# Low weight parts on GpSimd, and softmax division inside the transposing product, in an attention, MoE, MoE kernel

## The chip, the cores and the metric

The kernel runs on one core of one Trainium2 chip. The metric is the device time of one execution in microseconds, taken as the median of a few executions; lower is better. The profiled execution is one of them, recorded instruction by instruction.

## What is computed

Attention with a memory term (4 batches, 8 heads, 576 rows, 64 columns a head) gives a matrix of 2304 tokens by 512 columns. Two feed-forward layers (MoE 1 and MoE 2, each 512 to 2048 to 512) follow.

```python
scores = scale * q @ k.T                      # causal mask, B=4, H=8, S=576, D=64
a = exp(scores - scores.max(-1)); a /= a.sum(-1) + 1e-9
local = a @ v
q_p = where(q > 0, q, exp(q) - 1) + 1
mem_out = (q_p @ M_prev) / (q_p @ z_prev + 1e-6)
x = g * mem_out + (1 - g) * local             # g = sigmoid(beta), one per head
h = x @ w_in;  x = (h * sigmoid(h)) @ w_out   # MoE 1
h = x @ w_in2; out = elu(h) @ w_out2          # MoE 2
```

The weights arrive as 64-bit floating-point numbers, everything else as 32-bit ones.

## The kernel before

**Numbers in two parts.** The feed-forward products run on TensorE in a format with fewer mantissa bits (fp32r). Each operand is therefore kept as a high part (a copy in fp32r) and a low part (the number minus its high part), and three products (high by high, low by high, high by low) are summed. `split2` (L474) makes the two: ScalarE (ACT) copies the high part, VectorE (DVE) subtracts for the low part.

**Weights of MoE 1.** There are 32 tiles of 128 by 512: 16 of `w_in` (named `w0_0` to `w0_15`) and 16 of `w_out` (`w1_0` to `w1_15`). `w_stream` (L548) loads each as 64-bit integers into a landing tile (four landing places, which carry the names of the last tiles, such as `w0_14`). `w_value` builds the 32-bit number with one ACT and three DVE instructions (a TENSOR_SCALAR and two SCALAR_TENSOR_TENSOR on 128x512), and `w_split` (L543) calls `split2`: an ACT cast for the high part and a DVE TENSOR_TENSOR of 128x512 for the low part. The next load into a landing tile waits until the low part has read it.

**Attention.** Work is cut into tasks of a batch, a pair of heads and a region of rows. Batch 0 has two tasks for each of its four pairs: region A (rows 0 to 255) and region B (rows 256 to 575); the other batches have one task a pair (AB). `soft` (L729) does the scores of a task on TensorE (PE), the mask and the row minimum on DVE (a custom instruction, from PSUM), the exponential with row sums on ACT, the reciprocal of the sums on DVE, and then divides: the tiles called `e3` are scaled by ACT (`NORM = '3'`), all others (`eA`, `e2`, `e4`) by a DVE TENSOR_SCALAR. `a_T` (L789) and `b_T` (L802) transpose the divided tiles 128 columns at a time on PE, by a pass of the identity matrix (`ident`) over the tile; ACT copies the result out of PSUM (`a`), and `av_mm` multiplies it by the values. The result `x` of batch 0 is split at once and feeds MoE 1, whose blocks run woven into the attention of the later tasks.

**Order.** Nothing is issued in the order of the code. A planner (`Plan`) records all instructions, prices each with `Plan.cost`, schedules them on five engines in 24 forward and backward passes, and issues them in the order of its best pass. Each engine then works its instructions strictly in that order. A price in `Plan.cost` therefore moves instructions on all engines. Before the first weights are there, PE is given 70 small products of zeros as a filler.

GpSimd (POOL) does only memsets and masks here: 13 instructions in the first 3 us, and later one memset of 64x128 for each task.

Of the kernel before, what the change touches and what calls it, by code (L numbers as in the profile page):

```python
# [9 lines left out]
F32 = mybir.dt.float32  # L10
# [4 lines left out]
ALU = mybir.AluOpType  # L15
# [4 lines left out]
HP = 2000  # L20
OFF = 200
NORM = '3'
XHP = 1000
HOOK = 4
AHEAD = 4
# [132 lines left out]
class Plan:  # L158
# [82 lines left out]
    @staticmethod  # L241
    def cost(op, fn, args, kw, ins, outs, together):
        def cols(v):
            n = 1
            for m in v.shape[1:]:
                n *= m
            return n

        if op.eng == "PE":
            if fn == "transpose":  # L250
                return max(ins[0].shape[0] / 1.2, 0.84 * cols(ins[0]))
            n, m, once = cols(kw["rhs"]), cols(kw["lhsT"]), kw["rhs"].dtype != F32
            if together > 1:
                return n / (2.4 if together > 4 and kw["lhsT"].shape == (64, 64) else 1.2)
            return max(n / (2.4 if once else 0.6) + (13.5 if once else 3.0), 0.84 * m * (1 if once else 2))
        if op.eng == "DMA":
            v = outs[0] if isinstance(outs[0], View) else ins[0]
            n = 4
            for m in v.shape:
                n *= m  # L260
            return max(430.0, n / 280.0)
        n = cols(outs[0])
        psum = any(v.tile.space == "psum" for v in ins)
        if op.eng == "ACT":
            c = n / 1.2 + (51 if psum else 93) + (186 if kw.get("accum_out") is not None else 0)
            return c + (93 if isinstance(kw.get("scale"), View) else 0)
        if op.eng == "POOL":
            return n / 1.2 + 40
        if fn == "tensor_reduce":
            n = cols(ins[0])  # L270
        fast = fn in ("tensor_scalar", "tensor_copy") and not psum
        ptr = any(isinstance(kw.get(k), View) for k in ("scalar1", "scalar2")) or (
            fn == "scalar_tensor_tensor" and isinstance(kw["scalar"], View))
        return 69 + (60 if ptr else 0) + n / (1.92 if fast else 0.96)
# [125 lines left out]
def attention_moe_moe_kernel(  # L400
# [15 lines left out]
    nc = Plan(tc.nc)  # L416
    B, H, D, S = qT.shape
# [20 lines left out]
    def f32(ap):  # L438
        return ap.bitcast(F32)

    def new(pool, shape, dtype, tag, bufs=1):
        return nc.tile(pool, shape, dtype, tag, bufs, "psum" if pool is PP else "sbuf")
# [11 lines left out]
    def mm(o, l, r, start, stop):  # L454
        op = nc.tensor.matmul(o, lhsT=l, rhs=r, start=start, stop=stop, skip_group_check=True)
        pe[0] += op.cost
# [7 lines left out]
    def tr(o, i, ident):  # L464
        pe[0] += nc.tensor.transpose(o, i, ident).cost

    def sub(o, a, b):
        nc.vector.tensor_tensor(out=o, in0=a, in1=b, op=ALU.subtract)
# [2 lines left out]

        split2(t[:, 0], t[:, 1], src)

    def split2(hi, lo, src):  # L474
        nc.scalar.copy(hi, src)
        sub(lo, src, f32(hi))

    ident = new(at, [128, 128], F32, "ident")
    mask = new(at, [128, 704], BF16, "mask")
# [62 lines left out]

    def w_split(f, c, v):  # L543
        t = w_tile(f, c)
        split2(t[:, 512:1024], t[:, 0:512], f32(v))
        (win, wout)[c][f] = t

    def w_stream(srcs, ahead):  # L548
# [127 lines left out]

    tasks = [(b, p, r) for b in range(B) for r in (("AB",) if b else ("A", "B")) for p in range(NP)]
    qk_t, pr_t, e_t, pq_t, pt_t = {}, {}, {}, {}, {}
    x_done = set()

    def load(task):
        b, p, rg = task
# [46 lines left out]
    def soft(task, nms):  # L729


        b, p, rg = task
        small = new(at, [128, 12], F32, f"sm{nms}", 2)
        mx, su = small[:, 0:6], small[:, 6:12]
        rows = {"A": [(0, 0, 128), (1, 128, 256)], "2": [(2, 0, 384)], "3": [(3, 0, 512)]}
        parts, todo, tiles, col = [], [], [], 0
        if nms == "44":
            for i in range(2):
                t = (b, p - 1 + i, rg)
                e = e_t[t, 0, "4"] = new(at, [128, 576], F32, "e40", 2)  # L740
                k, c = 0, 2 * i
                for n, m0 in ((384, 0), (192, 512)):
                    s = ring()
                    parts.append((t, [s[0:64, 0:n], s[64:128, 0:n]], 512, 576, k, k + n))
                    todo.append((e[:, k:k + n], s[:, 0:n], m0, mx[:, c:c + 1] if k else 3e38,
                                 mx[:, c + 1:c + 2] if k else mx[:, c:c + 1]))
                    k += n
                tiles.append(("4", e, 0, 576, i, mx[:, c + 1:c + 2]))
            parts = parts[0::2] + parts[1::2]
            ogs = og[:, p - 1:p + 1, 2:3]  # L750
        else:
            per = sum(len(rows[nm]) for nm in nms)
            ogs = og[:, p, 0:2].unsqueeze(2)
        for nm in nms if nms != "44" else "":
            e = [new(at, [128, wide[nm]], F32, f"e{nm}{u}", 2 if nm in EDUP else 1) for u in range(2)]
            for u in range(2):
                e_t[task, u, nm] = e[u]
            s = [ring(), bank(f"acc{p % 2}") if rg == "A" else ring()]
            for qt, off, n in rows[nm]:
                parts.append((task, [s[u][:, off:off + n] for u in range(2)], qt * 128, qt * 128 + 128, 0, n))  # L760
            for u in range(2):
                for i, (qt, off, n) in enumerate(rows[nm]):
                    c = u * per + col + i
                    todo.append((e[u][:, off:off + n], s[u][:, off:off + n], 512 - n, 3e38, mx[:, c:c + 1]))
                    tiles.append((nm, e[u], off, n, c, mx[:, c:c + 1]))
            col += len(rows[nm])
        scores(parts)
        for x in todo:
            masked(*x)
        for nm, e, off, n, c, m in tiles:  # L770
            nc.scalar.activation(e[:, off:off + n], e[:, off:off + n], AF.Exp, scale=-1.0, bias=m,
                                 accum_out=su[:, c:c + 1])
        k = len(tiles)
        sv = su[:, 0:k].rearrange("p (u t) -> p u t", u=2)
        nc.vector.scalar_tensor_tensor(out=sv, in0=sv, scalar=1e-9, in1=ogs.to_broadcast([128, 2, k // 2]),
                                       op0=ALU.add, op1=ALU.mult)
        nc.vector.reciprocal(out=mx[:, 0:k], in_=su[:, 0:k])
        for nm, e, off, n, c, m in tiles:
            if nm in NORM:
                nc.scalar.activation(e[:, off:off + n], e[:, off:off + n], AF.Copy, scale=mx[:, c:c + 1])  # L780
            else:
                nc.vector.tensor_scalar(out=e[:, off:off + n], in0=e[:, off:off + n], scalar1=mx[:, c:c + 1],
                                        scalar2=None, op0=ALU.mult)

    def spread(t, c, u):

        return t[:, c:c + 256].rearrange("p (n h w) -> p n h w", h=2, w=64)[:, :, u, :]

    def a_T(task):  # L789

        res = []
        for u in range(2):
            a = new(at, [128, 384], F32, "a", ABUF)
            t = ring()
            for i in range(3):
                c = slice(i * 128, (i + 1) * 128)
                tr(t[:, c], e_t[task, u, "A"][:, c], ident[:])
            nc.scalar.copy(a[:], t[:, 0:384])
            res.append(a)
        return res  # L800

    def b_T(task, kt):  # L802


        a = new(at, [128, 640], F32, "a", ABUF)
        k = slice(kt * 128, (kt + 1) * 128)
        t = ring()
        if kt < 3:
            for u in range(2):
                tr(spread(t, 0, u), e_t[task, u, "2"][:, k], ident[:])  # L810
            tr(t[:, 256:384], e_t[task, 0, "4"][:, k], ident[:])
            nc.scalar.copy(a[:, 0:384], t[:, 0:384])
            t = ring()
            for u in range(2):
                tr(spread(t, 0, u), e_t[task, u, "3"][:, k], ident[:])
            nc.scalar.copy(a[:, 384:640], t[:, 0:256])
        else:
            tr(t[:, 0:128], e_t[task, 0, "4"][:, k], ident[:])
            for u in range(2):
                tr(spread(t, 128, u), e_t[task, u, "3"][:, k], ident[:])  # L820
            tr(t[:, 384:512], e_t[task, 0, "4"][:, 448:576], ident[:])
            nc.scalar.copy(a[:, 128:512], t[:, 0:384])
            nc.gpsimd.memset(a[0:64, 512:640], 0.0)
            nc.scalar.copy(a[64:128, 512:640], t[64:128, 384:512])
        return a
# [684 lines left out]
```

## Time and profile before

| what | value |
|---|---|
| median of 3 executions | 968.61 us (968.51 to 970.44) |
| profiled execution | 969.0 us |
| its span, first to last instruction | 967.1 us |
| TensorE clock granted | 1.00 throughout |
| PE busy | 951.3 us, 98% of the span |
| DVE busy | 725.7 us, 75% |
| ACT busy | 604.2 us, 62% |
| POOL busy | 5.9 us, 1% |

The share of an engine over the whole span hides stages, so the views that matter are the ones that cut the span: busy time by stretch, and the chain of work that ended last. A row of grouped instructions gives their count, their summed time and the mean of one; since an instruction may begin while the one ahead of it is still draining, the distance between two starts is shorter than the mean, and it is the distance that an instruction costs its engine.

### The profile page before, as it was taken

How to read it: one execution, taken by the hardware profiler on the slowest of the kernel's cores; microseconds unless marked ns; L12 is line 12 of the kernel's file. 1: busy time of each engine (PE TensorE's matmuls, PEld its weight loads, DVE VectorE, ACT ScalarE, POOL GpSimd, SP SyncE). 2: the span in 40 equal slices, each digit the busy share in tenths (PEclk: the TensorE clock that was granted, in tenths of full speed). 3: DMA queues.
4: the chain of work that ended last, by engine and by line, in shares of the span. 5: the costliest groups of instructions: out<-in, count | busy, mean ns of one | idle time of the engine just before them, and what ended most of it. 6: DMA issues, size and time to landing. Idle time of an engine off the chain costs nothing.

```text
span 967.1 us, 16218 instructions
## 1 busy us (share of the span) xinstructions
PE 951.3 (98%) x5862; PEld 824.6 (85%) x5862; DVE 725.7 (75%) x1629; ACT 604.2 (62%) x1292; POOL 5.9 (1%) x29
## 2 busy tenths in 40 slices
PE   8889999999999999999999999999999999999998
PEld 5467778777789989998999999898989989898987
DVE  7999999999859748765665578888898466548544
ACT  7998999999957456555545466555565344334321
POOL 1000000000000000000000000000000000000000
PEclk9999999999999999999999999999999999999999
DMA  7775456554321012334644435142421014003003
GB/s 212 243 208 178 128 150 197 162 165 139 90 82 35 1 44 93 140 122 148 207 152 131 154 119 163 55 142 77 142 88 44 1 34 120 1 17 116 32 0 109
DMA packets 101951, 107.36 MB, mean 111 GB/s; under 512 B 13040, under 2 KB 80624, under 8 KB 101872
## 3 DMA queue, kind: packets, MB, share of 16 engines
q1 hardware_dynamic: 101584, 106.07, 34.8%
q8 instruction: 46, 0.75, 0.3%
q14 instruction: 33, 0.27, 0.1%
q10 hardware_dynamic: 288, 0.26, 0.1%
HBM read 80.61 MB, written 25.69 MB: 110 GB/s over the span
## 4 chain that ended last, share of the span: by engine, by line
PE 90%; DVE 6%; ACT 2%; DMA 1%; issue 1%; SPq 0%; POOL 0%; DVEq 0%; ACTq 0%; POOLq 0%
PE b L201 49%; PE acc L201 17%; PE av L201 13%; PE h L201 11%; DVE w L201 2%; DVE x L201 1%; DVE eA L201 1%; DVE e L201 1%; ACT e L201 1%; DMA g<-xdB 1%; DVE qm L201 0%; DVE g L201 0%; ACT a L201 0%; DVE nm L201 0%; ACT L201 0%
## 5 line engine op out<-in xcount | busy, mean ns | idle before, releaser
L201 PE MATMUL b<-x,w 128*128 128x384 f32 (+1 forms) x1440 | 263.9, 325 | 0.1
L201 PEld LDWEIGHTS b<-x,w 128*128 128x128 f32 x1440 | 244.2, 188 | 10.8 <-ACT h L201 0.6
L201 ACT COPY x<-b 128x384 f32<-128x384 f32 (+2 forms) x144 | 67.3, 469 | 170.7 <-PE b L201 167.7
L201 DVE TENSOR_TENSOR h<-x,b 128x384 f32<-128x384 f32 (+1 forms) x128 | 66.1, 519 | 115.9 <-PE b L201 100.1
L201 PE MATMUL acc<-g,w 128*128 128x256 f32 (+1 forms) x720 | 146.1, 328 | 2.0 <-DVE g L201 1.1
L201 PEld LDWEIGHTS acc<-g,w 128*128 128x128 f32 x720 | 108.5, 190 | 15.8 <-issue 4.2
L201 PE MATMUL b<-x,g 128*128 128x256 f32 (+1 forms) x552 | 87.6, 301 | 0.0
L201 DVE SCALAR_TENSOR_TENSOR w<-w 128x512 int32<-128x512 int32 x124 | 84.1, 687 | 1.9
L201 PEld LDWEIGHTS b<-x,g 128*128 128x128 f32 x552 | 82.4, 189 | 3.2
L201 PE MATMUL acc<-w,g 128*128 128x512 f32 x288 | 81.0, 390 | 0.0
L201 PE MATMUL b<-w,g 128*128 128x512 f32 x288 | 74.8, 391 | 0.0
L201 ACT ACTIVATE g<-h 128x768 f32<-128x768 f32 x48 | 40.7, 848 | 48.3 <-DVE h L201 47.4
L201 ACT COPY a<-b 128x384 f32<-128x384 f32 (+2 forms) x160 | 62.6, 436 | 1.9 <-PE b L201 1.3
L201 ACT ACTIVATE e<-e,sm 128x512 f32<-128x512 f32 (+2 forms) x88 | 61.4, 718 | 2.9 <-DVE sm L201 2.7
L201 PEld LDWEIGHTS b<-w,g 128*128 128x128 f32 x288 | 53.9, 188 | 10.5
L201 PEld LDWEIGHTS acc<-w,g 128*128 128x128 f32 x288 | 53.7, 188 | 7.7
L201 DVE TENSOR_TENSOR g<-h,g 128x512 fp32r<-128x512 f32 (+1 forms) x48 | 37.4, 779 | 25.3 <-ACT g L201 25.1
L201 PE MATMUL b<-k,q 64*128 64x384 f32 (+5 forms) x368 | 55.1, 450 | 0.3
L201 ACT CAST g<-g 128x768 fp32r<-128x768 f32 x48 | 40.1, 836 | 17.1 <-DVE g L201 11.6
L201 PE MATMUL av<-a,vr 128*64 128x320 f32 (+4 forms) x448 | 50.3, 364 | 0.2 <-DVE x L201 0.2
L201 ACT CAST w<-w 128x512 fp32r<-128x512 f32 (+1 forms) x62 | 36.7, 597 | 19.9 <-DVE w L201 15.5
L201 PEld LDWEIGHTS av<-a,vr 128*64 128x64 f32 x448 | 29.3, 136 | 23.1 <-issue 2.1
(140 smaller groups left out, 1655.7 us busy)
## 6 DMA issues: line engine op xcount, KB each, us to landing
w<-in_moe_w_in SPq DMA_DIRECT2D x31, 512.0 KB, 4.0
w<-in_moe_w_out SPq DMA_DIRECT2D x31, 512.0 KB, 4.0
w1s<-g SPq DMA_DIRECT2D x32, 256.0 KB, 2.0
g<-w1s SPq DMA_DIRECT2D x32, 256.0 KB, 3.8
k<-in_kT SPq DMA_DIRECT2D x16, 288.0 KB, 4.2
qm<-in_qn SPq DMA_DIRECT2D x32, 128.0 KB, 3.0
vr<-in_vn SPq DMA_DIRECT2D x16, 256.0 KB, 3.3
q<-in_qT SPq DMA_DIRECT2D x12, 288.0 KB, 3.2
```

What stands on the lines that cost most here:

```text
L201: r = getattr(issue, fn)(*[a.make() if isinstance(a, View) else a for a in args], **{k: v.make() if isinstance(v, View) else v for k, v in ...
```

## The change

Three edits. First, the low parts of all 32 weight tiles of MoE 1 are subtracted on GpSimd instead of DVE (`LOW = 32`). Second, for batch 0 alone, the `eA` tiles of region A (divided by DVE before) and the `e3` tiles of region B (divided by ACT before) are not divided. Instead GpSimd scales the identity matrix by the reciprocals, one 128x128 diagonal matrix for each block of rows, and the transposing pass over `ident` becomes an ordinary fp32 product with that diagonal, which transposes and divides at once. There are 4 diagonals in each of the 4 A tasks and 2 in each of the 4 B tasks. They are kept in tiles that belong to the other region (`e30`, `e31` for A, `eA0`, `eA1` for B). Third, the planner's price of a GpSimd instruction rises from `n / 1.2 + 40` to `n * 1.6 + 150` ns.

```diff
+LOW = 32
+TURN = {"A": "A", "B": "3"}
...
         if op.eng == "POOL":
-            return n / 1.2 + 40
+            return n * 1.6 + 150
...
-    def split2(hi, lo, src):
+    def split2(hi, lo, src, eng=None):
         nc.scalar.copy(hi, src)
-        sub(lo, src, f32(hi))
+        (eng or nc.vector).tensor_tensor(out=lo, in0=src, in1=f32(hi), op=ALU.subtract)
...
-        split2(t[:, 512:1024], t[:, 0:512], f32(v))
+        split2(t[:, 512:1024], t[:, 0:512], f32(v), nc.gpsimd if 2 * f + c < LOW else None)
...
+    def turned(o, e, c, task, off=0):
+
+        d = turn_t.get(task, {}).get((e, off))
+        if d is None:
+            tr(o, e[:, c], ident[:])
+        else:
+            mm(o, e[:, c], d, True, True)
...
+        if nm in TURN.get(rg, ""):
+            w = new(at, [128, 4, 128], F32, f"e3{p % 2}", 2) if nm == "A" else new(at, [128, 3, 128], F32, f"eA{p % 2}", 2)
+            turn_t[task] = {}
+        slot = 0
         for nm, e, off, n, c, m in tiles:
-            if nm in NORM:
+            if nm in TURN.get(rg, ""):
+                d = turn_t[task][e, off] = w[:, slot]
+                slot += 1
+                nc.gpsimd.tensor_scalar(out=d, in0=ident[:], scalar1=mx[:, c:c + 1], scalar2=None, op0=ALU.mult)
+            elif nm in NORM:
...
-                tr(t[:, c], e_t[task, u, "A"][:, c], ident[:])
+                turned(t[:, c], e_t[task, u, "A"], c, task, 128 if i else 0)
...
-                tr(spread(t, 0, u), e_t[task, u, "3"][:, k], ident[:])
+                turned(spread(t, 0, u), e_t[task, u, "3"], k, task)
...
-                tr(spread(t, 128, u), e_t[task, u, "3"][:, k], ident[:])
+                turned(spread(t, 128, u), e_t[task, u, "3"], k, task)
```

**POOL, from its last mask on, before.** The names are tiles; `a` is the copy of a transposed block.

```order
L201 AFFINE_SELECT mask_0_101<-mask_0_101 64x64 x2
L201 MEMSET a_11_579 64x128
L201 MEMSET a_15_762 64x128
L201 MEMSET a_19_955 64x128
L201 MEMSET a_23_1266 64x128
```

The same place of POOL's queue now; `smA` and `sm23` hold the reciprocals of the row sums.

```order
L203 AFFINE_SELECT mask_0_101<-mask_0_101 64x64 x2
L203 TENSOR_SCALAR e30_0_256<-ident_0_107,smA_0_189 128x128 x4
L203 TENSOR_SCALAR e31_0_294<-ident_0_107,smA_1_219 128x128 x4
L203 TENSOR_SCALAR e30_1_382<-ident_0_107,smA_2_311 128x128 x4
L203 TENSOR_SCALAR e31_1_465<-ident_0_107,smA_3_354 128x128 x4
L203 TENSOR_TENSOR w0_0_0_461<-w0_14_0_154,w0_0_0_461 128x512
L203 TENSOR_TENSOR w0_1_0_567<-w0_15_0_324,w0_1_0_567 128x512
L203 TENSOR_SCALAR eA0_4_598<-ident_0_107,sm23_0_484 128x128 x2
L203 TENSOR_TENSOR w1_0_0_575<-w1_14_0_286,w1_0_0_575 128x512
L203 MEMSET a_11_622 64x128
```

All 16 diagonals of the A tasks stand ahead of the first low part, and the memset of an `a` tile stands behind low parts.

**DVE, behind the first A task's reciprocal, before.** `eA0` and `eA1` are the two heads' tiles of a task.

```order
L201 RECIPROCAL smA_0_189<-smA_0_189 128x4
L201 SCALAR_TENSOR_TENSOR qm_1_154<-em_1_227,qm_1_154 128x256
L201 TENSOR_SCALAR eA0_0_188<-eA0_0_188,smA_0_189 128x128
L201 TENSOR_SCALAR eA0_0_188<-eA0_0_188,smA_0_189 128x256
L201 TENSOR_SCALAR eA1_0_204<-eA1_0_204,smA_0_189 128x128
L201 TENSOR_SCALAR eA1_0_204<-eA1_0_204,smA_0_189 128x256
L201 TENSOR_TENSOR em_1_227<-qm_1_154,zb_1_217 128x256
```

And now:

```order
L203 RECIPROCAL smA_0_189<-smA_0_189 128x4
L203 ISA eA1_1_239,smA_1_219<-acc1_0_178,mask_0_101 128x256
L203 ISA smA_1_219 128x1
L203 TENSOR_TENSOR em_1_183<-qm_1_149,zb_1_185 128x256
L203 TENSOR_SCALAR og_0_236<-bet_0_140 64x4 x2
L203 TENSOR_REDUCE nm_1_270<-em_1_183 128x4
```

The four divisions are gone from DVE's queue, and the next instructions moved up.

**PE, at the first B task, before.** `h` is the first product of MoE 1, woven between the transposing passes (`b`).

```order
L201 MATMUL b2_6_583<-ident_0_103,e30_0_500 128x2x64
L201 MATMUL h_1_479<-x1_0_469,w0_0_0_457 128x256
L201 MATMUL b2_6_583<-ident_0_103,e31_0_507 128x2x64
L201 MATMUL b0_6_588<-ident_0_103,e30_0_500 128x2x64
L201 MATMUL b0_6_588<-ident_0_103,e31_0_507 128x2x64
```

And now:

```order
L203 MATMUL h_1_538<-x3_0_591,w0_0_0_461 128x256
L203 MATMUL b2_6_608<-eA0_4_598,e30_2_489 128x2x64
L203 MATMUL b0_6_611<-eA0_4_598,e30_2_489 128x2x64
L203 MATMUL b2_6_608<-eA0_4_598,e31_2_502 128x2x64
L203 MATMUL b0_6_611<-eA0_4_598,e31_2_502 128x2x64
L203 MATMUL b1_6_618<-ident_0_107,e20_0_495 128x2x64
```

The `e3` passes now read a diagonal (`eA0`), the `e2` passes still read `ident`, and the first tile's products of MoE 1 (`w0_0`) stand mostly ahead of them.

## Rows read from the trace of the kernel before

**Rows 1.** The page: busy time by engine, and PE by slices (tenths).

```profile
PE 951.3 (98%) x5862; PEld 824.6 (85%) x5862; DVE 725.7 (75%) x1629; ACT 604.2 (62%) x1292; POOL 5.9 (1%) x29
PE   8889999999999999999999999999999999999998
```

**Rows 2.** Busy time by stretch: length, PE, PEld, DVE, ACT, POOL, clock, DMA share, GB/s.

```profile
0.00:10.00 10.00, 8.24 (x75) 6.51 (x75) 4.71 (x29) 5.98 (x21) 2.44 (x13) 1.00 0.61 181
10.00:77.00 67.00, 57.80 (x410) 39.07 (x411) 66.51 (x205) 61.42 (x160) 0.85 (x4) 1.00 0.74 223
77.00:180.00 103.00, 102.85 (x823) 80.25 (x822) 100.77 (x343) 97.85 (x269) 1.19 (x6) 1.00 0.52 159
180.00:300.00 120.00, 119.81 (x962) 96.72 (x962) 105.12 (x334) 104.16 (x285) 1.44 (x6) 1.00 0.41 120
300.00:967.00 667.00, 662.63 (x3599) 602.04 (x3597) 448.61 (x723) 334.77 (x562) 0.00 (x0) 1.00 0.27 90
```

**Rows 3.** The chain that ended last, 72 to 82 us: start, length, what.

```profile
75.32 1.54 DVE w L201 x3
76.86 0.61 DVE g L201
77.47 0.04 issue
77.51 1.58 PE acc L201 x11
```

**Rows 4.** DVE's groups, 10 to 77 us: busy, mean ns, idle before.

```profile
L201 DVE SCALAR_TENSOR_TENSOR w<-w 128x512 int32<-128x512 int32 x26 | 17.7, 686 | 0.2
L201 DVE TENSOR_TENSOR w<-w,w 128x512 fp32r<-128x512 f32 x12 | 8.2, 680 | 0.0
...
L201 DVE TENSOR_SCALAR eA<-eA,smA 128x256 f32<-128x256 f32 x8 | 2.8, 344 | 0.0
...
L201 DVE TENSOR_SCALAR eA<-eA,smA 128x128 f32<-128x128 f32 x8 | 2.2, 281 | 0.0
...
L201 DVE TENSOR_TENSOR em<-qm,zb 128x256 f32<-128x256 f32 x3 | 1.2, 411 | 0.0
```

**Rows 5.** DVE's timeline near 10 and 64 us: start, length, instruction.

```profile
10.28 1.00 DVE L201 TENSOR_SCALAR eA<-eA,smA 128x128 f32<-128x128 f32 x4
11.20 0.42 DVE L201 TENSOR_TENSOR em<-qm,zb 128x256 f32<-128x256 f32 x1
...
64.36 0.69 DVE L201 TENSOR_TENSOR w<-w,w 128x512 fp32r<-128x512 f32 x1
64.97 0.55 DVE L201 TENSOR_TENSOR qm<-qm,nm 128x384 f32<-128x384 f32 x1
```

**Rows 6.** ACT's group of `e` tiles of 512 columns, 10 to 120 us.

```profile
L201 ACT ACTIVATE e<-e,sm 128x512 f32<-128x512 f32 x24 | 16.6, 716 | 0.1
```

**Rows 7.** PE's timeline near 130 us, and its group of diagonal products there.

```profile
129.64 0.71 PE L201 MATMUL b<-ident,e 128*128 128x128 f32 x5
...
130.31 0.70 PE L201 MATMUL av<-pt,diag 128*128 128x320 f32 x2
...
L201 PE MATMUL b<-ident,e 128*128 128x128 f32 x8 | 1.3, 272 | 0.0
L201 PE MATMUL av<-pt,diag 128*128 128x320 f32 x2 | 0.7, 432 | 0.0
```

**Rows 8.** POOL's timeline at the start: start, length, instruction.

```profile
0.81 0.69 POOL L201 MEMSET mask<- 128x704 bf16 x1 [0.29 <-POOLq L1500]
...
1.96 0.29 POOL L201 TENSOR_SCALAR_AFFINE_SELECT ident<-ident 128x128 f32<-128x128 f32 x1
```

**Rows 9.** Two memsets of POOL and what DVE did beside each.

```profile
255.72 0.45 POOL L201 MEMSET a<- 64x128 f32 x1 [13.30 <-PE av L201]
255.61 0.77 DVE L201 TENSOR_SCALAR e<-e,smA 128x384 f32<-128x384 f32 x2
...
169.65 0.20 POOL L201 MEMSET a<- 64x128 f32 x1 [17.19 <-ACT t L201]
169.39 0.42 DVE L201 SCALAR_TENSOR_TENSOR qm<-em,qm 128x256 f32<-128x256 f32 x1
169.72 0.68 DVE L201 SCALAR_TENSOR_TENSOR w<-w 128x512 int32<-128x512 int32 x1
```

**Rows 10.** PE's group with the most idle time, 10 to 77 us.

```profile
L201 PE MATMUL h<-x,w 128*128 128x256 f32 x73 | 12.6, 303 | 3.8 <-DVE t L201 1.3 <-DVE w L201 1.2 <-ACT w L201 0.9
```

More of the change, by code (lines that the diff above doesn't have):

```diff
@@ L678, in attention_moe_moe_kernel @@
     qk_t, pr_t, e_t, pq_t, pt_t = {}, {}, {}, {}, {}
+    turn_t = {}
     x_done = set()
+    def turned(o, e, c, task, off=0):
[4 more added lines that the diff above has]
+            mm(o, e[:, c], d, True, True)
     def load(task):
```

## The prediction

> **What bounds the kernel now.** I read four views, from coarse to fine. The page first: PE is busy for 951.3 of 967.1 us, and its slices are full from the fourth on [rows 1]. So only the first 75 us or so can hold anything but PE work. Then the busy time by stretch [rows 2]: from 10 to 77 us DVE is busy 66.51 of 67.00 us and PE only 57.80, so PE idles for 9.2 us there. From 77 to 180 us PE has 102.85 of 103.00 us, from 180 to 300 us 119.81 of 120. Third, the chain of work that ended last: it lies on DVE up to 76.86 us (making weights, then a `g`), and passes to PE at 77.51 us [rows 3]. That gives the rule for this change: **up to 77 us the time is what DVE needs; behind 77 us every us added to PE is a us of time, and nothing taken from DVE helps.** The most that any relief can bring is the 9.2 us of idle, less what PE gets to do in addition. The profiled execution took 969.0 us, 0.4 above the median of 968.61; I count from 969.0.
>
> **Part 1, PE's products.** A task of region A has 6 transposing passes over `eA`, a task of region B 8 over `e3`, and there are four of each: 24 + 32 = 56 passes become products. Five passes in a row take 0.71 us, of which the last one's own length is 0.272, so they start (0.71 - 0.27) / 4 = 0.11 us apart [rows 7]. An fp32 product has two records: the 320-column one takes 0.70 us in all with a mean of 0.432, so its second half starts 0.27 us behind the first, which is 0.84 ns a column and half [rows 7]. For 128 columns that is 0.107 us a half, 0.214 for the product. Each product adds about 0.107 us, all 56 add **6.0 us of PE work**. No row speaks for less.
>
> **Part 2, what DVE is rid of up to 77 us.** Twelve low parts lie there [rows 4]. One holds the queue from 64.36 to 64.97 us, 0.61 us [rows 5]; twelve make 7.3 us. The 16 divisions of region A (8 of 256 columns, 8 of 128 [rows 4]) run in fours; four hold the queue from 10.28 to 11.20, 0.92 us [rows 5], so 3.7 us. Together **11.0 us** out of 67.
>
> **Part 3, what ACT is rid of.** Eight divisions of 512 columns at some 0.716 us (the row has exponentials and divisions together [rows 6]), 5.7 us. ACT had 61.42 us of work in the 67 [rows 2] and does not end the chain there [rows 3], so I count nothing for it; it keeps ACT from becoming late when DVE gets faster.
>
> **Part 4, what POOL gets, and what DVE pays for it.** Up to 77 us POOL gets 16 diagonals of A, 6 of the first three B tasks and 12 low parts. The nearest row of a diagonal is the 128x128 affine select of `ident`, 0.29 us [rows 8]: 22 x 0.29 = 6.4 us. A low part has 512 columns; from below, the memset of 704 columns in 0.69 us gives 0.50 us, from above four affine selects of 128 give 1.17 [rows 8]. I take the middle, 0.85: 12 x 0.85 = 10.2 us. POOL is then busy for 16.6 of 67 us; it was idle, so that alone costs nothing, and its memsets of `a` wait behind one or two low parts at most.
>
> The question is whether POOL's work slows DVE. One memset took 0.45 us where the others take 0.20, and it stood beside two TENSOR_SCALARs of DVE from SBUF to SBUF; another beside two-operand instructions took its usual 0.20 [rows 9]. So the two engines do block each other on some pairs. A memset reads nothing; no row shows a POOL instruction that reads tiles beside DVE. The stall is bounded by nothing at all and by POOL's whole time. The twelve low parts' own companions in DVE's queue are what decides: of DVE's groups from 10 to 77 us, eleven are TENSOR_SCALARs of tiles or have two SBUF operands (the largest 17.7 us, the smallest 1.2 [rows 4]), in sum 38.2 of the 68.4 us that are left without the low parts and divisions, 56%. The rest reads PSUM or a single tile. I take it that DVE stands still when POOL works and such an instruction is next: 0.56 x 16.6 = 9.3 us. I prefer this to nothing because the one row in which POOL and DVE met on tiles shows a wait of a whole instruction, not a small slowdown. DVE's net is then -11.0 + 9.3 = **-1.7 us**, with the ends -11.0 and, at 1.17 a low part and a full stall, 12 x 1.17 + 6.4 - 11.0 = +9.4.
>
> [...]
>
> **Part 5, where the added PE work lies.** All 24 products of A and those of three B tasks, 48 x 0.107 = 5.1 us, fall before 77 us, where PE has 9.2 us of idle; the last 8, 0.9 us, fall where it has none. The cover is not complete: the products stand between the softmax and `x`, and PE's idle ends with waits on DVE's `t` and `w` and ACT's `w` [rows 10], so a product that delays `a` and `x` delays DVE's split of `x` and what follows. I take half, **2.6 us**, with the ends 0 and 5.1.
>
> **Part 6, order.** The new queues put products of MoE 1 further ahead of the passes of the first B tasks. If a low part from POOL is late, PE stands at it with passes queued behind; landing tiles also come free later, by the difference of 0.85 and 0.61 us, and the load into them with it. I count nothing, since the relief of DVE lets the three instructions ahead of a low part run earlier, and keep it as a rival.
>
> **Sum.** -1.7 (DVE's stage) + 2.6 + 0.9 = +1.8 us: 970.8. Its own range, with the stall at 0.45 to 0.7 of POOL's time (-3.5 to +0.6 for DVE) and the cover from 0 to 5.1, and without both ends at once: 967.5 to 974.
>
> **Rivals.**
> Rival 1, POOL and DVE do not hinder each other when both read. For it: the memset beside two-operand instructions that took its usual 0.20 us [rows 9]. Then DVE is 11.0 us lighter, PE becomes the bound almost from the start, and the idle goes: -9.2 + 6.0 = -3.2 us if all of it goes, -11.0 + 6.0 = -5.0 if DVE's relief counts in full, since the filler products and waits hidden in PE's busy time also shrink. I put it at -4.0: **965.0**, 962.5 to 967.5. Faster.
> Rival 2, each POOL instruction stops DVE for its whole length: 16.6 - 11.0 = +5.6 for DVE, with 3.5 for PE as above: +9.1, **978**, 974 to 982. It decides from a stall of 0.66 of POOL's time on (11.0 / 16.6), where DVE's stage stops getting shorter; in a stretch dense in weights, where two-operand instructions follow each other, that is near. Against it: a third of DVE's time reads PSUM and can run beside POOL.
> Rival 3, the low parts come late on an in-order PE: the idle ahead of `h`, 3.8 us [rows 10], doubles. With no change on DVE's net: 969.0 + 0.9 + 3.8 + 2.6 - 1.7 = **974.6**.
>
> **How the numbers follow.** Forecast 0.42, rival 1 0.36, rival 2 0.14, rival 3 0.08. A difference of 0.2% (1.9 us) is about what a measurement of this kernel can tell from no change: below 966.7 is faster, above 970.5 slower. The forecast gives 0.03 to faster, 0.19 to the same, 0.20 to slower; rival 1 gives 0.32 to faster, 0.04 to the same; rivals 2 and 3 all to slower. Faster 0.35, same 0.23, slower 0.42. The range from 963 to 977 leaves out a little of rival 1 at the bottom and most of rival 2 at the top, some 0.17.
>
> **What would show each step.** In the profile after: 32 low parts and 24 diagonals on POOL, and their mean lengths (0.85 and 0.29 taken); the start distance of the new products (0.214); the mean of DVE's SCALAR_TENSOR_TENSOR on weights, 686 ns before: unchanged under rival 1, well above it if POOL blocks DVE; the point at which PE stops idling (77 us before: earlier under rival 1, about the same under the forecast, later under rival 2). What would make it wrong: a low part far shorter than 0.85 us, or a stall that the order of the queues avoids.

## The result, and the profile after

The changed kernel takes **981.99 us** (median of 4 executions, 981.47 to 983.34); the kernel before, run beside it, 969.23. The ratio is 1.0133, with a 95% interval of 1.0115 to 1.0150: 12.8 us slower. The forecast was 970.8 with a range of 963 to 977, so the side was the one given the largest chance and the size was missed. The profiled execution took 983.34 us, with a span of 981.3.

The page of after: busy time by engine, and the 40 slices of PE, POOL and the granted clock in tenths.

```profile
PE 961.0 (98%) x5918; PEld 837.5 (85%) x5918; DVE 729.8 (74%) x1581; ACT 601.9 (61%) x1284; POOL 69.0 (7%) x85
PE   8898999999999999999999999999999999999998
POOL 4543101220000000000000000000000000000000
PEclk9998999999999999999999999999999999999999
```

Against [rows 1], PE's busy time is 9.7 us longer and its idle time 4.5 us (20.3 against 15.8). DVE, which lost 32 subtractions and 16 divisions, is busier than before, 729.8 against 725.7 us. The same stretches as [rows 2], in the same columns (length, PE, PEld, DVE, ACT, POOL, clock, DMA share, GB/s), and below them four short ones:

```profile
0.00:10.00 10.00, 6.33 (x44) 4.75 (x45) 3.43 (x18) 4.63 (x14) 2.42 (x13) 1.00 0.54 167
10.00:77.00 67.00, 60.70 (x475) 46.99 (x475) 63.08 (x175) 54.96 (x146) 35.27 (x38) 1.00 0.70 212
77.00:180.00 103.00, 98.78 (x770) 78.12 (x768) 99.14 (x302) 92.85 (x250) 17.77 (x19) 0.97 0.51 152
180.00:300.00 120.00, 117.68 (x919) 90.83 (x916) 100.89 (x337) 105.75 (x298) 13.55 (x17) 0.99 0.39 120
...
77.00:81.00 4.00, 1.85 (x9) 0.72 (x5) 3.93 (x7) 2.38 (x5) 1.35 (x2) 0.92 0.72 237
81.00:87.00 6.00, 5.65 (x26) 5.65 (x27) 5.60 (x16) 3.84 (x10) 0.00 (x0) 0.50 0.36 118
214.00:217.00 3.00, 0.69 (x5) 0.49 (x5) 3.00 (x9) 0.58 (x3) 1.90 (x3) 0.98 0.06 18
217.00:220.00 3.00, 3.00 (x12) 2.59 (x13) 2.93 (x10) 2.84 (x12) 0.00 (x0) 0.50 0.45 160
```

PE now idles behind 77 us, where it was full before: 4.2 us up to 180 and 2.3 us up to 300. Twice the granted clock falls to 0.50 right behind such idle time: from 81 to 87 us after four us in which PE was busy for 1.85, and from 217 to 220 us after three in which it was busy for 0.69. POOL is busy for 35 of the 67 us from 10 to 77, where the prediction had 16.6.

What happens at 77 us stands in the timeline (start, length, engine, instruction), only DVE, POOL and PE shown:

```profile
75.40 1.67 POOL L203 TENSOR_TENSOR w<-w,w 128x512 fp32r<-128x512 f32 x1 [1.14 <-ACT w L203]
75.86 1.76 DVE L203 SCALAR_TENSOR_TENSOR w<-w 128x512 int32<-128x512 int32 x1
...
79.46 1.28 POOL L203 TENSOR_TENSOR w<-w,w 128x512 fp32r<-128x512 f32 x1 [2.39 <-ACT w L203]
79.49 1.80 DVE L203 TENSOR_TENSOR g<-t,g 128x512 fp32r<-128x512 f32 x1
...
81.35 0.58 PE L203 MATMUL acc<-g,w 128*128 128x256 f32 x1 [1.17 <-DVE g L203]
```

A POOL low part begins, and the DVE instruction that begins beside it takes 1.76 or 1.80 us in place of 0.69 and 0.68; it ends 0.55 us behind POOL. The second one is the low part of a `g` for which PE waits. The chain that ended last runs through both, where in [rows 3] it ran through the same kinds of instructions at their usual length:

```profile
75.86 1.76 DVE w L203
77.62 0.46 DVE nm L203
...
79.49 1.81 DVE g L203
81.30 0.04 issue
81.35 0.58 PE acc L203
```

Not every DVE instruction is held. Masks, which read PSUM, run beside a low part at their usual length, 0.55 us:

```profile
47.12 1.49 POOL L203 TENSOR_TENSOR w<-w,w 128x512 fp32r<-128x512 f32 x1 [3.65 <-ACT w L203]
...
47.38 0.55 DVE L203 CUSTOM_DVE_ANT_0 e<-b,mask 128x384 f32<-128x384 f32 x1
```

By groups (busy, mean ns, idle before), DVE and POOL of after from 10 to 77 us:

```profile
L203 DVE SCALAR_TENSOR_TENSOR w<-w 128x512 int32<-128x512 int32 x27 | 22.7, 849 | 0.3
L203 DVE CUSTOM_DVE_ANT_0 e<-b,mask 128x384 f32<-128x384 f32 x10 | 5.3, 548 | 0.0
...
L203 POOL TENSOR_TENSOR w<-w,w 128x512 fp32r<-128x512 f32 x13 | 18.3, 1410 | 18.2 <-ACT w L203 16.6 <-DMA w<-in_moe_w_in 1.5
L203 POOL TENSOR_SCALAR e<-ident,smA 128x128 f32<-128x128 f32 x16 | 11.3, 724 | 12.7 <-DVE smA L203 10.0 <-DMA k<-in_kT 2.8
L203 POOL TENSOR_SCALAR eA<-ident,sm 128x128 f32<-128x128 f32 x6 | 5.4, 912 | 7.7 <-DVE sm L203 7.7
```

The weight products of DVE average 849 ns against 686 in [rows 4]. Adding up, over the whole trace, what DVE's instructions took beyond the usual length of their kind (for those over by more than 0.08 us) gives 20.4 us, 8.2 of them before 77 us. Of the 20.4, 19.8 us stand beside low parts: 0.62 us for each of the 32, about the 0.61 us that each one saved.

### The profile page after: what moved, and what is told of

Read it like the earlier page. It is cut to its first block, busy times and chain, and to the rows that moved or that the text cites. A ratio compares the mean times of both kernels' runs of the same rounds, so it can differ in the third digit from the quotient of the medians.

```text
span 981.3 us, 16409 instructions
## 1 busy us (share of the span) xinstructions
PE 961.0 (98%) x5918; PEld 837.5 (85%) x5918; DVE 729.8 (74%) x1581; ACT 601.9 (61%) x1284; POOL 69.0 (7%) x85
## 4 chain that ended last, share of the span: by engine, by line
PE 85%; DVE 5%; ACT 3%; issue 2%; DMA 2%; POOL 1%; SPq 0%; DVEq 0%; ACTq 0%; POOLq 0%
PE b L203 48%; PE acc L203 17%; PE av L203 11%; PE h L203 9%; DVE w L203 2%; ACT a L203 1%; DVE e L203 1%; POOL e L203 1%; ACT e L203 1%; DMA xdB<-pt 1%; DMA k<-in_kT 1%; DMA zb<-in_z_prev 1%; DVE qm L203 0%; ACT w L203 0%; DVE g L203 0%
## 5 line engine op out<-in xcount | busy, mean ns | idle before, releaser
L203 DVE SCALAR_TENSOR_TENSOR w<-w 128x512 int32<-128x512 int32 x124 | 89.5, 733 | 2.2
L203 ACT ACTIVATE e<-e,sm 128x512 f32<-128x512 f32 (+2 forms) x80 | 56.1, 717 | 4.8 <-DVE sm L203 4.6
```

The lines of the kernel that those rows point to most:

```text
L203: r = getattr(issue, fn)(*[a.make() if isinstance(a, View) else a for a in args], **{k: v.make() if isinstance(v, View) else v for k, v in ...
```

## The experiments

Three theories stood at the start. L: a GpSimd instruction that reads SBUF stops DVE's instructions with two tile operands. P: the loss is the added PE work of the products. O: the loss is the new order. Times are medians, ratios are to the kernel before, run on the same chip at the same time, with the 95% interval.

**The parts apart.** Low parts alone (`e1_low`), diagonals and products alone (`e2_diag`), the planner's price alone (`e3_price`); each is planned anew.

```diff
-TURN = {"A": "A", "B": "3"}      # e1_low; in e3_price as well
+TURN = {}
-LOW = 32                         # e2_diag; in e3_price as well
+LOW = 0
```

> The low parts alone on GpSimd, all divisions as before (new price, new order). [...] Theory P (the loss is the added PE work of the products): no products, so within 2 us of before or faster. Theory O (the loss is the new order): 3 us or more over before, with DVE's instructions at their usual lengths.

> The diagonals and their products alone, low parts on DVE as before (new price, new order). Theory P: 5 to 7 us over before. Theory L: 24 diagonals of 0.6 us stop DVE for 5 to 10 us less 3.7 us of divisions, together with the products 4 to 9 us over before. Theory O gives no number of its own here.

> Only the planner's price of a GpSimd instruction is new; every instruction is the one of before, but some 600 rows of PE's queue stand elsewhere. This measures what another order is worth by itself. Theories L and P: within 2 us of before. Theory O: 3 us or more away from before.

Measured: `e1_low` 981.96 us (1.0125, 1.011 to 1.014), `e2_diag` 970.29 (1.0009, 0.9999 to 1.0018), `e3_price` 969.30 (0.9996, 0.9986 to 1.0006). The whole loss, 12.4 us, is in the low parts; P falls, and the price alone costs nothing though it reorders PE's queue. POOL's diagonals in `e2_diag` from 5 to 260 us, and DVE's weight products there from 10 to 77:

```profile
L203 POOL TENSOR_SCALAR e<-ident,smA 128x128 f32<-128x128 f32 x16 | 10.2, 652 | 13.4 <-DVE smA L203 13.4
L203 POOL TENSOR_SCALAR eA<-ident,sm 128x128 f32<-128x128 f32 x8 | 9.3, 1176 | 46.6 <-DVE sm L203 43.3 <-ACT w L203 3.3
...
L203 DVE SCALAR_TENSOR_TENSOR w<-w 128x512 int32<-128x512 int32 x27 | 18.3, 685 | 0.0
```

DVE keeps its 685 ns; a diagonal takes 0.65 us in the mean in the A tasks and 1.18 in the B tasks, where the shortest in after took 0.60, so here, as far as the lengths tell, it is POOL that waits. L's 4 to 9 us didn't come: beside the diagonals, which read SBUF too, DVE's instructions are over their usual length by 0.6 us in all.

**Products alone, in the order of before.** The 56 passes become fp32 products with `ident`, and the divisions stay.

```diff
+        if task[2] != "AB":
+            op.run = lambda: nc.nc.tensor.matmul(o.make(), lhsT=i.make(), rhs=ident.make(), start=True, stop=True,
+                                                 skip_group_check=True)
```

> Queues of all engines exactly as before, all divisions as before; the 56 transposing passes are issued as fp32 products with the identity. Nothing goes to GpSimd. Price by the prediction: 6.0 us of PE work, of which 3.5 us (0.9 behind 77 us, 2.6 uncovered) show: 972 to 973. Theory P (all of it shows): 975. If all of what lies ahead of 77 us is covered: 970.

Measured: 970.81 us (1.0011, 1.0002 to 1.002). The added PE work, priced at 6.0 us, cost 1.1 us.

**The hold by itself.** `e5_queue` keeps the order of before on PE, ACT and the DMA queues and moves only the 32 subtractions from DVE's queue to POOL's. `e6_spare` leaves them on DVE and adds a second, unused subtraction on POOL for each. `e7_memset` adds two POOL memsets of 128x512 in its place.

```diff
+        nc.add("vector", [("tensor_tensor", (), dict(out=lo, in0=src, in1=f32(hi), op=ALU.subtract))], "gpsimd")   # e5_queue
...
+            nc.nc.gpsimd.tensor_tensor(out=dead.make(), in0=src.make(), in1=f32(hi).make(), op=ALU.subtract)       # e6_spare
...
+            for _ in range(2):                                                                                     # e7_memset
+                nc.nc.gpsimd.memset(dead.make(), 0.0)
```

> The low parts are issued on GpSimd, but the order of every queue is that of before (the planner still takes them for DVE instructions); no products. Theory L: DVE loses 32 x 0.6 us of its own and is stopped for about as long or longer, 1 to 7 us over before. Theory O (only the new order hurts): 969 or faster, down to 963, as DVE is 7 us lighter up to 77 us. Lateness alone (a low part arrives 0.7 us later on an in-order PE): up to 4 us over before with DVE at its usual lengths.

> Queues as before, low parts on DVE as before; beside each of the 32, GpSimd subtracts the same two operands once more into the dead half of the landing tile, which no one reads. Only the next load into that place waits for it. Theory L: DVE is stopped with nothing taken off it; up to 77 us 12 x 1.27 us of GpSimd, so 6 to 15 us over before, two-operand DVE instructions at 1.0 to 1.8 us. Without a block between the engines: 969, DVE at its usual lengths, unless a load comes late (up to 3 us).

> As the run with spare subtractions, but GpSimd writes the dead half twice with zeros (two memsets of 128x512) and reads nothing. Theory L in the narrow form (a GpSimd instruction that reads stops two-operand instructions, one that only writes stops TENSOR_SCALARs alone): SCALAR_TENSOR_TENSORs on weights keep their 690 ns, TENSOR_SCALARs get longer, 0 to 3 us over before. If writing alone stops all of them: as the spare subtractions.

Measured: `e5_queue` 976.06 us (1.0062, 1.0047 to 1.0077), `e6_spare` 992.45 (1.0230, 1.0215 to 1.0246), `e7_memset` 970.7 (1.0010, 1.0000 to 1.0019). POOL work that DVE needs nothing of costs 22.7 us in `e6_spare`, above the 6 to 15 that L gave for the first 77 us alone; there DVE's own low parts average 1105 ns against 680 in [rows 4]:

```profile
L201 DVE TENSOR_TENSOR w<-w,w 128x512 fp32r<-128x512 f32 x10 | 11.1, 1105 | 0.0
...
L552 POOL TENSOR_TENSOR w<-w,w 128x512 f32<-128x512 f32 x30 | 44.3, 1478 | 133.6 <-ACT w L201 109.8 <-issue 23.7
```

The memsets of `e7_memset` are nearly as long together (two of 556 ns) and cost a us; DVE's weight products stay at 688 ns. L holds for the subtraction. In the old order the loss is half of that in the new one, so something of O is left.

**A planner that knows POOL's length.** The whole change, with a price of 1.42 us for a low part and 0.75 for a diagonal.

```diff
-            return n * 1.6 + 150
+            return n * 1.75 + 376 + 150
```

> The whole change, with the planner told 1.42 us for a low part and 0.75 us for a diagonal instead of 0.97 and 0.35. Theory O (the order rests on prices that are too low): at least 6 of the 12.8 us come back, 976 or less. Theory L (DVE is stopped, which the planner doesn't know at any price of GpSimd): 978 to 986.

Measured: 979.94 us (1.0102, 1.0085 to 1.0119). Two us better, three by the ratio: the right price for POOL doesn't help much. That the cost falls on DVE, where the planner has none, fits this but isn't shown by it. The granted clock in this trace is 1.00 from 10 to 300 us, where the changed kernel has 0.97 and 0.99 behind 77 us, so part of the two or three us may be the clock's.

**Another kind of POOL instruction.** `e9_one_old` (order of before) and `e10_one_new` (order of `e1_low`) write the low part with a one-input operation, high part times zero.

```diff
+        op.run = lambda: nc.nc.gpsimd.tensor_scalar(out=lo.make(), in0=f32(hi).make(), scalar1=0.0, scalar2=None, op0=ALU.mult)
```

> The queue order of the kernel before, all 32 low parts on GpSimd, but written as a one-input operation (high part times zero, 128x512) in place of the subtraction of two; the true low part is left out, so the products with it add zeros. GpSimd keeps the place in the order, the waits and the buffers of e5_queue (976.06 us). Theory L (GpSimd's two-input subtraction stops VectorE's two-operand instructions): a one-input operation does not, VectorE's 128x512 products stay near 690 ns up to 77 us and VectorE is freed of 0.61 us a low part; the time falls to 963 to 969 us, the first rival of the prediction. Theory Q (what costs is that the low parts come late, or that a foreign engine stands in the chain): the time stays at 974 to 977 us. If GpSimd's own length is more than 1.3 us, the one-input form was held in its turn, and low parts come later.

> As e9_one_old (one-input operation on GpSimd for each low part, the true low part left out), but in the order of e1_low (981.96 us), which was planned for VectorE without the low parts. L: the plan's assumption now holds, VectorE's products at about 690 ns, 960 to 968 us. O (the new order is bad in itself): 974 us or more, with PE idle in the same places as in e1_low.

Measured: `e9_one_old` 968.58 us (0.9994, 0.9983 to 1.0005), `e10_one_new` 971.55 (1.0019, 1.001 to 1.0028). In `e9_one_old` a low part of POOL takes longer than in `e5_queue` (1.57 us in the mean, against 1.38), stands at the same place, and the 6 us are gone; lateness (theory Q) falls. Its timeline shows DVE instructions with tile operands at their usual length inside a POOL instruction, and below them one that is held:

```profile
38.29 2.94 POOL L548 TENSOR_SCALAR w<-w 128x512 fp32r<-128x512 f32 x2 [2.49 <-ACT w L201]
...
39.08 0.56 DVE L201 SCALAR_TENSOR_TENSOR qm<-em,qm 128x384 f32<-128x384 f32 x1
...
46.18 1.55 POOL L548 TENSOR_SCALAR w<-w 128x512 fp32r<-128x512 f32 x1 [4.80 <-ACT w L201]
...
46.83 0.43 DVE L201 TENSOR_SCALAR w<-w 128x512 int32<-128x512 int32 x1
...
62.94 1.56 POOL L548 TENSOR_SCALAR w<-w 128x512 fp32r<-128x512 f32 x1 [0.67 <-ACT w L201]
63.08 1.09 DVE L201 SCALAR_TENSOR_TENSOR w<-w 128x512 int32<-128x512 int32 x1
```

The first two begin 0.79 and 0.65 us behind the start of the POOL instruction. The third begins 0.14 us behind it and takes 1.09 us in place of 0.69: it ends as if it had been let go 0.54 us into the 1.56. So here the one-input form held DVE as well, but only at its beginning, where the subtractions above held it to their end (the 1.76 and 1.80 us).

`e10_one_new` met neither expectation (960 to 968, or 974 and more). And neither run came near the 963 us that the relief of DVE was priced at. That opened the second question: what is the relief worth?

**Where the hold costs.** `e12_late` gives POOL only the 18 low parts after the 14th, `e15_early` only the first 14; the order is that of before.

```diff
+               "gpsimd" if 2 * f + c >= 14 else "vector")     # e12_late; < 14 in e15_early
```

> The queue order of the kernel before; only the low parts after the 14th, those that are made after about 77 us, go to GpSimd's queue, the first 14 stay on VectorE. By the prediction's rule that nothing on VectorE counts behind 77 us: 968.5 to 970 us. If VectorE is close enough to the bound until 180 us that an instruction held for a us stops PE's suppliers: 971 to 975 us, and most of e5_queue's 6.3 us lies here; the rest of it then belongs to the first 77 us.

> The queue order of the kernel before; only the first 14 low parts, those made before about 77 us, go to GpSimd as real subtractions, the other 18 stay on VectorE: the complement of e12_late (972.55, +3.2). If the two parts add up to e5_queue's +6.3: 971.5 to 973.5 us. If hold and saving balance up to 77 us: 969 to 970 us, and e5's loss would need both parts at once.

Measured: `e12_late` 972.55 us (1.0030, 1.0019 to 1.0041), `e15_early` 972.67 (1.0027, 1.0018 to 1.0036). They add up to `e5_queue`'s loss. `e12_late` refutes the rule that nothing on DVE counts behind 77 us. Its largest single loss:

```profile
180.47 1.28 POOL L201 TENSOR_TENSOR w<-w,w 128x512 fp32r<-128x512 f32 x1
180.69 1.48 DVE L201 SCALAR_TENSOR_TENSOR qm<-em,qm 128x384 f32<-128x384 f32 x1
182.10 1.27 POOL L201 TENSOR_TENSOR w<-w,w 128x512 fp32r<-128x512 f32 x1 [0.35 <-ACT w L201]
182.56 1.22 DVE L201 TENSOR_TENSOR em<-qm,zb 128x384 f32<-128x384 f32 x1
183.71 0.34 DVE L201 TENSOR_SCALAR eA<-eA,smA 128x256 f32<-128x256 f32 x1
184.11 0.44 PE L201 MATMUL b<-ident,eA 128*128 128x128 f32 x2 [1.08 <-DVE eA L201]
```

Two instructions of 0.55 us are held to 1.48 and 1.22 us, the division behind them is late, and PE stands for 1.08 us in a stretch where it never stood before.

**What the relief is worth, and what the order is worth.** `e11_order` issues the low parts on DVE, in the order planned for GpSimd. `e13_zero_old` and `e14_zero_new` set them to zero by a POOL memset, in the old and the new order. `e16_none_old` and `e17_none_new` leave them out, and PE reads the high part twice, so PE's work is the same.

```diff
+        nc.add("gpsimd", [("tensor_tensor", (), dict(out=lo, in0=src, in1=f32(hi), op=ALU.subtract))], "vector")   # e11_order
...
+        op.run = lambda: nc.nc.gpsimd.memset(f32(lo).make(), 0.0)     # e13_zero_old, e14_zero_new
...
+        op.run = lambda: None                                         # e16_none_old, e17_none_new
+        if i and w in bare:
+            v.make = w[:, 512:1024].make
```

> The order of e1_low, planned as though GpSimd made the low parts, but each low part issued on VectorE's queue at its place in that order. Nothing runs on GpSimd that did not before. If the order planned for a lighter VectorE costs by itself the 6 us between e5_queue and e1_low: 973 to 979 us, with PE idle between 77 and 82 us. If the 6 us need the GpSimd subtraction too: 969 to 972 us.

> The queue order of the kernel before; each of the 32 low parts is set to zero by a GpSimd memset (128x512) in place of the subtraction, so the true low part is left out. VectorE is freed of 32 x 0.61 us with nothing that stops it (the same memsets cost e7_memset 1 us beside unchanged VectorE durations) and the low parts come earlier than in e9_one_old, whose one-input operation took 1.59 us. If the first 77 us are VectorE's alone, as the prediction had it: 958 to 963 us. If another engine is as near (PE 86%, ScalarE 92% busy there): 966 to 968.5 us, and e9's gain of 0.8 us was nearly all that there is.

> As e13_zero_old (memsets in place of the low parts, the true low part left out), in the order of e1_low, which was planned for just such a VectorE. If the order is good where what it assumes holds: at or below e13_zero_old. If it is bad in itself: 2 to 4 us above e13_zero_old, as e10_one_new stands above e9_one_old.

> The queue order of the kernel before with the 32 low parts left out altogether: no engine makes them, and TensorE reads the high part a second time in the products that took the low part, so TensorE's work is the same and the true low part is left out. VectorE is freed of 32 x 0.61 us and GpSimd does nothing that it did not before: the worth of the relief alone, without any hold. If VectorE alone sets the time up to 77 us, as the prediction had it: 959 to 963 us. If TensorE is full from about 63 us on and only what it idles before then can be won: 965.5 to 968 us. Above 969 us the relief would be worth nothing at all.

> As e16_none_old (low parts left out altogether, the high part read twice), in the order of e1_low, which was planned for a VectorE without them. If that order is good where its assumption holds exactly: at or below e16_none_old. If it is bad in itself: 2 to 4 us above e16_none_old, which is then the price of the order alone, and e1_low's further 10 us belong to the hold.

Measured, with the earlier runs beside them:

| low parts made by | order of before | order planned for GpSimd |
|---|---|---|
| nobody | `e16_none_old` 967.28 (0.9977, 0.9968 to 0.9987) | `e17_none_new` 968.79 (0.9994, 0.9984 to 1.0003) |
| POOL, one input | `e9_one_old` 968.58 | `e10_one_new` 971.55 |
| POOL, memset | `e13_zero_old` 971.79 (1.0024, 1.0014 to 1.0033) | `e14_zero_new` 970.41 (1.0009, 0.9999 to 1.0018) |
| DVE | before, 968.6 to 969.8 | `e11_order` 980.09 (1.0101, 1.0085 to 1.0116) |
| POOL, subtraction | `e5_queue` 976.06 | `e1_low` 981.96 |

Taking all 32 low parts away from DVE, with nothing in exchange, is worth **2.2 us** in the old order by its ratio (2.4 by the medians), and in the new order 0.6 us against the kernel before, which the interval doesn't tell from nothing. The new order is no very bad order where its assumption holds (1.5 us behind the old, less than the 2 to 4 that would have made it bad in itself). With the low parts put back on DVE it costs 11.3 us more, in the old order 2.4: the planner filled DVE's freed time with other work, and what is put back then presumably stands on the chain (`e11_order` came out just above the 973 to 979 us that were expected). In the new order a hold of 0.62 us a low part costs nearly the same as putting it back (981.96 against 980.09). In the old order it doesn't: the subtractions at their planned places on DVE cost 2.4 us, as holds 8.8.

`e13_zero_old` missed its expectation for a reason of its own: seven memsets ran in a row, and three divisions beside them, usually 0.41 us each, took 4.37.

```profile
44.83 4.37 DVE L201 TENSOR_SCALAR e<-e,sm 128x384 f32<-128x384 f32 x3
44.91 3.32 POOL L548 MEMSET w<- 128x512 f32 x7
...
50.40 0.33 PE L201 MATMUL b<-ident,e 128*128 128x128 f32 x1 [3.36 <-DVE sm L201]
```

Why the clean relief is worth so little is seen in `e16_none_old` and in the kernel before, cut at the point where PE stops waiting. First before, then `e16_none_old`:

```profile
10.00:63.80 53.80, 44.70 (x310) 27.84 (x310) 53.31 (x177) 49.46 (x133) 0.85 (x4) 1.00 0.75 225
63.80:77.00 13.20, 13.10 (x100) 11.23 (x101) 13.20 (x30) 11.96 (x28) 0.00 (x0) 1.00 0.71 214
```

```profile
10.00:63.30 53.30, 46.16 (x313) 28.41 (x311) 49.90 (x170) 49.60 (x135) 0.82 (x4) 0.97 0.74 228
63.30:77.00 13.70, 13.70 (x105) 11.83 (x106) 13.23 (x31) 12.31 (x30) 0.00 (x0) 1.00 0.82 260
```

And two lines of the timeline of `e16_none_old`, the `g` that ended the chain in [rows 3] and the first PE product that reads it:

```profile
74.41 0.69 DVE L201 TENSOR_TENSOR g<-t,g 128x512 fp32r<-128x512 f32 x1 [0.37 <-ACT g L201]
76.61 1.48 PE L201 MATMUL acc<-g,w 128*128 128x256 f32 x11
```

All but 0.1 us of PE's idle time between 10 and 77 us lies before 63.8 us; from there on DVE *and* PE are full. Before that point the idle time is 9.1 us, and without any low part it is still 7.1: the 2.0 us between them are what the relief brings. That `g` began at 76.78 us before and begins 2.4 us earlier now; it is ready 1.5 us before PE comes to it, and PE comes to it at 76.61 instead of 77.51, only 0.9 us earlier. Before 63 us PE's waits on ACT and on the chain through softmax stay; ACT was busy for 92% of that time. The 20 to 23 us stretch of `e16_none_old` also has a granted clock of 0.55, where before has 1.00; that may take back part of what was won, and what PE did in the us ahead of it doesn't differ enough to say why.

## Why the prediction missed

- **What bounds the kernel: this step failed, at both ends.** The rule took a DVE that is 99% busy up to 77 us as the bound. From 63.8 us on PE was full as well, and before that the idle belonged only in part to DVE. Behind 77 us, DVE is at 98% (100.77 of 103 us, [rows 2]) and some of its instructions feed PE just in time, so a hold of a us can reach PE: `e12_late`, +2.9 us by its ratio where the rule had nothing.
- **Part 2, DVE's relief (11.0 us counted in full): mis-sized.** All 32 low parts, not twelve, are worth 2.2 us when they vanish (`e16_none_old`). No hold was in that run, and it stands at 967.28, at the upper end of rival 1's range and not at its 965.0. The 16 divisions are still on DVE there; no run takes both away without a hindrance, but `e2_diag`, with the divisions gone and the products added, is no faster than before (970.29).
- **Part 4, POOL's lengths: mis-sized.** A low part takes 1.27 us at the least and 1.41 in the mean up to 77 us, against 0.85 (and above the upper bound of 1.17); a diagonal 0.60, and in the mean 0.72 (A) and 0.91 (B), against 0.29. The affine select and the memset were no good rows for arithmetic on tiles.
- **Part 4, the hold: right in sum up to 77 us by luck, since two errors cancelled.** It gave 9.3 us, the trace 8.2. But POOL worked 35 us there, not 16.6, and nearly all the holding was done by the subtractions (0.62 us each); beside diagonals alone the same sum gives 0.6 us in all 24 of `e2_diag`. That POOL would stop DVE's instructions with two tile operands stood in no row of before; it was the author's estimate, and beside the subtractions it came true (1.76 and 1.80 us beside 1.67 and 1.28). The one-input operations of `e9_one_old` read tiles too, and there it came true only in part: one held a two-operand instruction at its beginning (1.09 in place of 0.69 us), another did not hold one that began later in it (0.56 us, as usual).
- **Part 5, the products (3.5 us): too dear.** `e4_product` measured 1.1 us where 3.5 were expected to show, and beside the low parts they cost nothing that can be seen (981.99 against 981.96). The start distance was right: four records in 0.61 us with a mean of 283 ns are 0.11 us apart.
- **Part 6, the order (nothing): the largest error, 5.9 us (`e1_low` over `e5_queue`).** It is 1.5 us by itself (`e17_none_new` against `e16_none_old`), but it makes the hold dearer: 13.2 us in the new order (`e1_low` over `e17_none_new`) against 8.8 in the old (`e5_queue` over `e16_none_old`); by the ratios 12.7 and 8.2. So the 12.4 us of `e1_low` are about -0.9 for the relief in its order and +13.2 for the hold and POOL's length.
- **The sum, by medians.** Forecast: -7.3 us for the low parts' relief, -0.2 for divisions and products together (-3.7 and +3.5), +9.3 for the hold, nothing for the order: +1.8. Measured: -2.4 (`e16_none_old`), +0.7 (`e2_diag`), +8.8 for the hold over the whole run, +5.9 for the order, together 13.0 where the change cost 12.8. So the relief, 4.9 us too large, and the order, 5.9 us left out, make the miss.
- **Rival 2** had what the subtractions were seen to do (978, POOL stops DVE for its whole length; 1.76 and 1.80 us in place of 0.69 and 0.68) and stopped at 77 us; it left out the 12.2 us of holds behind that point and counted 16.6 us ahead of it, where the trace has 8.2. That 981.99 lies inside its 974 to 982 is luck. **Rival 3**, late low parts, is out: `e9_one_old` is as late and loses nothing.

The lower clock is a small part of the 13.2 us. The same columns as above, first `e1_low`, then `e17_none_new`:

```profile
10.00:77.00 67.00, 54.86 (x408) 40.82 (x406) 65.08 (x189) 55.62 (x145) 15.87 (x14) 0.95 0.67 204
77.00:180.00 103.00, 100.31 (x791) 77.84 (x792) 98.40 (x299) 95.51 (x258) 20.18 (x18) 1.00 0.53 161
```

```profile
10.00:77.00 67.00, 58.83 (x446) 42.79 (x445) 63.37 (x204) 60.16 (x159) 0.79 (x4) 0.97 0.72 225
77.00:180.00 103.00, 103.00 (x825) 80.16 (x825) 96.55 (x328) 99.66 (x274) 0.99 (x5) 1.00 0.54 161
```

By an estimate in which PE's work stretches as the clock falls, a clock of 0.95 over 67 us is 3.4 us and one of 0.97 is 2.0, so the clock can explain about 1.5 us of the difference. `e3_price` has 0.95 there as well and lost nothing, and the trace of `e8_true` has 1.00 and that run lost 10.1 us. What grew is PE's idle time: some 26 us in all in `e1_low` against 18 in `e17_none_new`, and 4.8 of the 8 us lie between 77 and 300 us.

Open: why the same 20 us of DVE's time cost 2.4 us as its own subtractions and 8.8 as holds in the old order. `e12_late` shows one hold that falls on an instruction for which PE stands; that the others cost their time in the same way is argued.

## What to carry to other kernels

Before work is moved to another engine, time the instruction there and look at what it does to the instructions of the engine that is to be relieved: 32 subtractions saved 0.61 us each on DVE and held it for 0.62. An engine at 99% is the bound only where the engine behind it waits; cut the stretch where that one's idle time ends before pricing any relief. And where a planner sets the order, a work item that it believes gone and that comes back, as itself (11.3 us against 2.4) or as a hold (13.2), costs several times what it cost before.

## What the runs showed of the hardware

- A two-input POOL subtraction of 128x512 took 1.27 us at the least and 1.39 in the mean (after), and held DVE instructions with two tile operands until it ended (1.76 and 1.80 us in place of 0.69 and 0.68), and a DVE TENSOR_SCALAR of a tile too (1.57 us in place of 0.41, from 34.96 us on in after). A mask, which reads PSUM, passed (0.55 us, from 47.38 us on).
- A one-input POOL operation of the same tile took longer, 1.57 us in the mean (`e9_one_old`), and held DVE far less: 5.4 us in 32 by the same sum that gives 20.4 in the changed kernel, with weight products of 737 ns in the mean from 10 to 77 us against 849. An instruction that began 0.14 us behind its start was let go some 0.54 us into it; those that began 0.65 and 0.79 us behind it took their usual time (0.43 and 0.56 us).
- Beside seven POOL memsets in a row (3.32 us) three DVE TENSOR_SCALARs took 4.37 us (`e13_zero_old`); in `e7_memset`, with two memsets to each low part, DVE's weight products stayed at 688 ns.
- The granted clock stood at 0.50 from 81 to 87 us in after, behind four us of which PE had idled for 2.2.
